# Rounds of half a batch with all heads, key products on VectorE, and weights decoded by integer bits, in a fused RWKV6 attention and MLP kernel

## The chip, the cores and the metric

The kernel runs on one core of one Trainium2 chip. The metric is the device time of one execution in microseconds (us), the median of several runs. A run over 1.5% above the fastest of its kernel is called slow, the others fast; only fast runs are compared, while medians and ranges given here are of all runs. A core has TensorE (matmuls), VectorE, ScalarE and GpSimd (elementwise work), and SyncE, which here issues transfers. In the profile they are PE (PEld is its weight load), DVE, ACT, POOL and SP. "L304" is line 304 of the kernel concerned; the kernel before and the changed one number their lines differently.

## The reference

Four batches, eight heads, 768 steps, 48 channels a head. The recurrence runs over the steps; its output, with the heads side by side, is the input x of a normalised two-layer MLP over 4 x 768 = 3072 tokens.

```python
for t in range(S):                       # per batch and head; state is 48 x 48
    cur = u * k[t] (outer) v[t]
    y[t] = r[t] @ (state + cur)
    state = w[t][:, None] * state + k[t] (outer) v[t]
x  = y.transpose(0, 2, 1, 3).reshape(B, S, H * D)          # 3072 x 384
xn = (x - mean(x)) / sqrt(var(x) + 1e-6) * g_ln
out = x + maximum(xn @ w_ch1, 0) @ w_ch2                    # 384 -> 1536 -> 384
```

The MLP weights reach the kernel as 64-bit floats, as pairs of 32-bit words, and are turned into 32-bit floats on the chip, in 24 pieces of 128 x 384.

## The kernel before

Attention is done in chunks of 64 steps. Inside a chunk six levels halve the steps: at level n the later half of each block reads from the earlier half (one set of matmuls, 96 in a round as the trace counts them), then R and K are multiplied by the decay products of their blocks. A unit is two heads by 768 steps, a round is two units. The levels of a round run beside the ends of the round before (kn transposes, states, outputs), the transposes of the round after, and pieces of the MLP as filler. The MLP of a batch needs all eight heads, hence two rounds.

```python
units = [(b, g) for b in range(B) for g in range(G)]      # g: a pair of heads, all 768 steps
...
    # a level, after its matmuls, for both units of the round
    POOL.tensor_tensor(out=K[:, :, 0, :], in0=K[:, :, 0, :], in1=T[:, :, 1]..., op=ALU.mult)   # L296
    DVE.tensor_tensor(out=R[:, :, 1, :], in0=R[:, :, 1, :], in1=T[:, :, 0]..., op=ALU.mult)    # L300
    # then copy_predicated (masked) from PSUM to A on VectorE, L313
...
    # decoding of one piece: exponent, mantissa, product
    DVE.tensor_scalar(out=e, in0=hi, ... shift 20, and 0x7FF)
    ACT.activation(out=e, in_=e, func=AF.Relu, bias=bias)                # bias -896
    DVE.tensor_scalar(out=e, in0=e, ... min 255, mult 2**23)
    DVE.scalar_tensor_tensor(out=e, in0=hi, ... sign bit, in1=e)
    DVE.tensor_scalar(out=m, in0=hi, ... and 0xFFFFF)
    ACT.activation(out=m, in_=m, func=AF.Copy, bias=1.0, scale=2.0**-20)
    DVE.scalar_tensor_tensor(out=m, in0=lo, scalar=2.0**-52, in1=m, ...)
    POOL.tensor_tensor(out=dst, in0=m, in1=e, op=ALU.mult)
...
    # the MLP of 384 tokens: statistics, 9 transposes, then the h matmuls and the o matmuls
    # (the trace counts 72 of each)
```

## Time and profile before

| What | Kernel before |
|---|---|
| time, median of 3 runs | 722.87 us (722.41 to 725.46) |
| first h matmul of the MLP | 193.2 us |
| from there to the end of the profiled span (724.5 us) | 531.3 us |
| busy: TensorE, VectorE, ScalarE, GpSimd | 616.1, 309.5, 190.0, 259.9 us |

The page gives the busy time of each engine and its course over 40 slices of the span; what matters here is the moment at which the MLP's first matmul can start, because from there on TensorE hardly ever waits. So I cut each profile at that matmul: the stretch from 20 us to it is called the start (the first 20 us are loads and set-up), the stretch behind it the rest. The prediction below shows the lines of before. The same cut at exactly the first h matmul; columns are the stretch, its length, then busy time (and instructions) of PE, PEld, DVE, ACT and POOL, the granted TensorE clock, DMA share and GB/s:

```profile
20.00:193.17 173.17, 96.40 (x2452) 83.00 (x2452) 145.55 (x260) 63.87 (x131) 125.72 (x130) 0.63 0.52 114
193.17:724.50 531.33, 505.80 (x5873) 325.83 (x5871) 159.22 (x348) 119.13 (x259) 115.33 (x127) 0.96 0.12 26
```

In the start TensorE is busy for 96 of 173 us, at a mean clock of 0.63; VectorE is busy for 146.

### The profile page before, as it was taken

To read this page: it belongs to the slowest core of one execution; us is meant where nothing else is said; L and a number is where in the kernel's file an instruction comes from. 1 tells how busy PE (TensorE), PEld (TensorE's weight loads), DVE (VectorE), ACT (ScalarE), POOL (GpSimd) and SP (SyncE) were. 2 spreads that over 40 slices of the span, in tenths; PEclk is the share of its full clock that TensorE was granted. 3 is DMA by queue.
4 is the path that set the end of the run, shared out by engine and by line. 5 is a ranking of instruction groups with operands and counts; after the bars stand their busy time and mean duration, and the time that the engine had idled before them with its cause. 6 is when DMAs were issued, how large, how long until landed. Compare 5 with 4: busy or idle time off the path is not lost.

```text
span 724.5 us, 18947 instructions
## 1 busy us (share of the span) xinstructions
PE 616.1 (85%) x8456; PEld 419.2 (58%) x8456; DVE 309.5 (43%) x612; ACT 190.0 (26%) x402; POOL 259.9 (36%) x301
## 2 busy tenths in 40 slices
PE   6632655568799989997999999999999999799998
PEld 4522545557456666676566666676666566455554
DVE  1479999896605332345306242556053012400000
ACT  3142453341522114213212241124210420220210
POOL 9975786775405142336104161533012100000000
PEclk9975565655799989997799999996999999999999
DMA  9919438532202330225002520000000000000000
GB/s 158 225 27 201 116 82 181 118 67 50 44 1 46 70 70 2 38 58 90 1 1 46 104 36 1 24 23 10 1 13 24 2 1 23 12 1 22 12 0 33
DMA packets 120688, 36.80 MB, mean 51 GB/s; under 512 B 114336, under 2 KB 117536, under 8 KB 120608
## 3 DMA queue, kind: packets, MB, share of 16 engines
q1 hardware_dynamic: 120608, 35.60, 24.2%
q8 instruction: 66, 1.08, 0.6%
q14 instruction: 14, 0.11, 0.1%
HBM read 30.87 MB, written 4.72 MB: 49 GB/s over the span
## 4 chain that ended last, share of the span: by engine, by line
PE 67%; DVE 19%; POOL 5%; issue 4%; ACT 3%; DMA 1%; POOLq 0%; SPq 0%; DVEq 0%
PE h_ps L429 25%; PE o_ps L439 23%; PE a_ps L286 9%; DVE rT L300 3%; DVE A L313 3%; DVE we L206 2%; DVE s L351 2%; PE xT_ps L420 2%; DVE wm L210 2%; DVE wm L214 2%; PE y L372 2%; DVE we L198 1%; DVE we L203 1%; PE y L382 1%; ACT A L311 1%
## 5 line engine op out<-in xcount | busy, mean ns | idle before, releaser
L429 PE MATMUL h_ps<-xT,w_sb 128*128 128x384 f32 x576 | 199.2, 506 | 1.3 <-ACT h L434 1.0
L439 PE MATMUL o_ps<-w_sb,h 128*128 128x384 f32 x576 | 193.3, 488 | 0.0
L296 POOL TENSOR_TENSOR kT<-kT,tot 128x384 f32<-128x384 f32 x80 | 89.3, 1128 | 207.3 <-PE a_ps L286 207.0
L429 PEld LDWEIGHTS h_ps<-xT,w_sb 128*128 128x128 f32 x576 | 112.2, 198 | 79.4 <-issue 8.0
L286 PE MATMUL a_ps<-rT,kT 48*64 48x32 f32 x4608 | 106.3, 247 | 58.3 <-DVE A L313 39.8
L439 PEld LDWEIGHTS o_ps<-w_sb,h 128*128 128x128 f32 x576 | 106.8, 190 | 68.2
L286 PEld LDWEIGHTS a_ps<-rT,kT 48*64 48x64 f32 x4608 | 97.6, 166 | 83.9 <-issue 57.8
L300 DVE TENSOR_TENSOR rT<-rT,tot 128x384 f32<-128x384 f32 x80 | 62.1, 780 | 148.0 <-PE a_ps L286 145.5
L434 ACT ACTIVATE h<-h_ps 128x384 f32<-128x384 f32 x96 | 46.7, 490 | 141.1 <-PE h_ps L429 141.1
L445 DVE TENSOR_TENSOR o<-o_ps,x 128x384 f32<-128x384 f32 x24 | 13.4, 557 | 164.4 <-PE o_ps L439 164.3
L313 DVE COPY_PREDICATED A<-mask,a_ps 128x384 f32<-128x384 int8 x80 | 55.1, 750 | 0.0
L351 DVE SCALAR_TENSOR_TENSOR s<-s,decay,kv 128x48 f32<-128x48 f32 x160 | 42.0, 263 | 4.7
L358 ACT COPY sx<-s 64x288 f32<-64x288 f32 x32 | 13.7, 430 | 100.3 <-DVE s L351 100.0
L217 POOL TENSOR_TENSOR w_sb<-wm,we 128x384 f32<-128x384 f32 x24 | 31.0, 1299 | 19.6 <-DVE wm L214 12.1
L372 PE MATMUL y<-v,A 64*64 64x48 f32 x384 | 26.9, 232 | 6.5 <-DVE s L351 5.3
L296 POOL TENSOR_TENSOR kT<-kT,wT 128x384 f32<-128x384 f32 x16 | 21.7, 1363 | 27.2 <-PE a_ps L286 19.7
L233 ACT COPY rT<-r_ps 128x384 f32<-128x384 f32 x32 | 13.9, 480 | 66.4 <-PE r_ps L229 41.7
L372 PEld LDWEIGHTS y<-v,A 64*64 64x64 f32 x384 | 24.7, 146 | 8.2 <-issue 8.2
L256 POOL TENSOR_TENSOR rk<-nat_k,nat_r 128x576 f32<-128x576 f32 x16 | 23.3, 1458 | 16.8 <-PE a_ps L286 8.2
L372 PE MATMUL y<-vx,A 64*64 64x48 f32 x384 | 26.3, 232 | 1.5 <-issue 1.5
L421 ACT ACTIVATE xT<-xT_ps,g_sb 128x384 f32<-128x384 f32 x24 | 13.1, 578 | 54.7 <-PE xT_ps L420 54.6
L342 PE MATMUL kv<-v,kn 64*64 64x48 f32 x768 | 19.6, 246 | 9.2 <-DVE s L351 5.4
(59 smaller groups left out, 652.5 us busy)
## 6 DMA issues: line engine op xcount, KB each, us to landing
raw<-in_moe_w_ch_dram SPq DMA_DIRECT2D x24, 384.0 KB, 4.5
nat_w<-in_w_dram SPq DMA_DIRECT2D x32, 144.0 KB, 3.9
nat_k<-in_k_dram SPq DMA_DIRECT2D x32, 144.0 KB, 3.5
nat_r<-in_r_dram SPq DMA_DIRECT2D x32, 144.0 KB, 4.2
v<-in_v_dram SPq DMA_DIRECT2D x32, 144.0 KB, 3.9
out_dram<-o SPq DMA_DIRECT2D x24, 192.0 KB, 1.9
vx<-in_v_dram SPq DMA_DIRECT2D x32, 72.0 KB, 3.5
u_bc<-in_u_dram SPq DMA_DIRECT2D x1, 192.0 KB, 4.3
```

The lines of the kernel that those rows point to most:

```text
L217: POOL.tensor_tensor(out=dst, in0=m, in1=e.bitcast(F32), op=ALU.mult)
L256: POOL.tensor_tensor(out=rk, in0=nat["k"][q % 2][:, :, :, 0:D], in1=nat["r"][q % 2][:, :, :, 0:D], op=ALU.mult,)
L286: PE.matmul(ps[ds(C * (i ^ j), C), j, u, c].rearrange("s (q n) -> s q n", n=n), K[rows, ts(m, C)], R[rows, m, :, 1, :], start=True, stop=True,
L296: POOL.tensor_tensor(out=K[:, :, 0, :], in0=K[:, :, 0, :], in1=T[:, :, 1][:, :, None].broadcast_to(blocks), op=ALU.mult,)
L300: DVE.tensor_tensor(out=R[:, :, 1, :], in0=R[:, :, 1, :], in1=T[:, :, 0][:, :, None].broadcast_to(blocks), op=ALU.mult,)
L313: DVE.copy_predicated(out=out_j[:, :, 1, :], mask=masks[lev], data=ps_j)
L342: PE.matmul(kv[ds(HP * j, HP), i, c], a["kn"][ds(C * i, C), c, ds(HP * j, HP)], vn[q][ds(C * i, C), c, j, :], start=True, stop=True,)
L351: DVE.scalar_tensor_tensor(out=s[:, m, :], in0=s[:, m - 1, :], scalar=a["T"][NLEV][:, m : m + 1], in1=new, op0=ALU.mult, op1=ALU.add,)
L372: PE.matmul(y[ds(C * i, C), j, c], A[rows, j, q % 2, c, :], vx[q][rows, c] if j else vn[q][rows, c, j], start=c == 0, stop=c + i == 0, ski ...
L429: PE.matmul(ps, w1_sb[:, kc, ts(f, P)], xT[:, kc, :], start=kc == 0, stop=kc == KC - 1,)
L434: ACT.activation(out=hs[f], in_=ps, func=AF.Relu)
L439: PE.matmul(ps, hs[f][:, ts(i, P)], w2_sb[:, f, :], start=f == 0, stop=f == FC - 1)
```

## The change

The intent: start the MLP after one round, not two, and take work off the two engines that hold up the start. A unit becomes four heads by 384 steps; two units, all eight heads, make a round that ends in 384 finished tokens. The state at step 384 is carried to the second half. The K products go from GpSimd to VectorE. Decoding works on the integer bits: ScalarE scales the absolute high word and converts the low word, VectorE clamps, shifts and sets the sign, and GpSimd adds the low bits as an integer. Further: unit 1's loads are issued by ScalarE, the mask copies move from GpSimd to ScalarE, raw weights come into three buffers of one piece, the three PSUM uses of attention share two buffers, and x rows are copied once per MLP to be contiguous.

```diff
-    units = [(b, g) for b in range(B) for g in range(G)]
+    rounds = [(b, f) for b in range(B) for f in range(NHALF)]
+    units = [(b, f, g) for b, f in rounds for g in range(U)]
...
+    load(0)
+    load(1, ACT)
...
-            POOL.tensor_copy(
+            ACT.copy(
                 out=half[rows],
...
-            e = ph.tile([P, WC], I32, tag="h", name=f"we{i}")
-            m = ph.tile([P, WC], F32, tag="h", name=f"wm{i}")
+            e = p3.tile([P, WC], I32, tag="we", name=f"we{i}")
+            low = p2.tile([P, WC], I32, tag="wl", name=f"wl{i}")
+            ACT.activation(
+                out=e.bitcast(F32), in_=hi.bitcast(F32), func=AF.Abs, scale=2.0**-16
+            )
+            ACT.activation(out=low, in_=lo, func=AF.Copy, scale=2.0**-29)
             DVE.tensor_scalar(
-                out=e, in0=hi, scalar1=20, scalar2=0x7FF,
-                op0=ALU.logical_shift_right, op1=ALU.bitwise_and,
-            )
-            ...
+                out=e.bitcast(F32), in0=e.bitcast(F32), scalar1=2.0**-31,
+                scalar2=1.875 - 2.0**-23, op0=ALU.max, op1=ALU.min,
+            )
+            DVE.tensor_scalar(
+                out=e, in0=e, scalar1=3, scalar2=0x7FFFFFF8,
+                op0=ALU.logical_shift_left, op1=ALU.bitwise_and,
+            )
             DVE.scalar_tensor_tensor(
                 out=e, in0=hi, scalar=-(1 << 31), in1=e,
                 op0=ALU.bitwise_and, op1=ALU.bitwise_or,
             )
-            ...
-            POOL.tensor_tensor(out=dst, in0=m, in1=e.bitcast(F32), op=ALU.mult)
+            POOL.tensor_tensor(out=dst.bitcast(I32), in0=e, in1=low, op=ALU.add)
...
-            POOL.tensor_tensor(
-                out=K[:, :, 0, :], in0=K[:, :, 0, :],
-                in1=T[:, :, 1][:, :, None].broadcast_to(blocks), op=ALU.mult,
-            )
-            DVE.tensor_tensor(
-                out=R[:, :, 1, :], in0=R[:, :, 1, :],
-                in1=T[:, :, 0][:, :, None].broadcast_to(blocks), op=ALU.mult,
-            )
+            for nm, i in (("r", 1), ("k", 0)):
+                X = a[nm].rearrange("p (q two n) -> p q two n", two=2, n=n)[:, :, i, :]
+                DVE.tensor_tensor(
+                    out=X, in0=X, in1=T[:, :, 1 - i][:, :, None].broadcast_to(blocks),
+                    op=ALU.mult,
+                )
...
+            DVE.tensor_copy(out=xn[i], in_=x[:, :, i, :])
```

## The prediction

> **What bounds the kernel now.** First I read the page: busy shares, and the 40 slices (18.1 us each).
>
> ```profile
> PE 616.1 (85%) x8456; PEld 419.2 (58%) x8456; DVE 309.5 (43%) x612; ACT 190.0 (26%) x402; POOL 259.9 (36%) x301
> ...
> PE   6632655568799989997999999999999999799998
> ...
> DVE  1479999896605332345306242556053012400000
> ...
> POOL 9975786775405142336104161533012100000000
> PEclk9975565655799989997799999996999999999999
> ```
>
> There are two stages. In slices 2 to 10 TensorE is busy half the time, at half clock in places, while VectorE reads 9. From slice 11 TensorE reads 9. The busy times of the engines in three stretches give the cut exactly; the columns are the stretch, its length, then PE, PEld, DVE, ACT and POOL busy, then PEclk:
>
> ```profile
> 20.00:192.00 172.00, 95.23 (x2446) 82.25 (x2445) 144.38 (x258) 63.52 (x130) 124.55 (x130) 0.64 0.53 115
> 192.00:623.00 431.00, 409.79 (x5577) 269.46 (x5575) 154.70 (x337) 104.27 (x229) 116.50 (x127) 0.95 0.14 29
> 623.00:724.50 101.50, 97.18 (x305) 57.12 (x305) 5.69 (x13) 15.21 (x31) 0.00 (x0) 0.98 0.03 12
> ```
>
> So 192 us pass before the first MLP matmul; then 431 us of TensorE at 95%; then 101 us of pure MLP. The chain that ended last gives MLP prices (start, us, what):
>
> ```profile
> 193.24 23.08 PE h_ps L429 x66
> ...
> 649.22 23.23 PE o_ps L439 x72
> 674.30 23.49 PE h_ps L429 x72
> ```
>
> 384 tokens cost 23.5 + 23.2 + 2.5 (nine transposes with evacuations) = 49 us of TensorE, eight times: 394 us that no reordering removes. Attention, from the same chain at full clock, costs per round of 1536 head-steps in two units: 6 levels x 1.53, 36 transposes of w, k, r x 0.152 = 5.5, kn 1.6, kv 1.7, y 2.6; about 20.6 us, eight times.
>
> The first stage is where time lies. TensorE there waits for VectorE:
>
> ```profile
> 60.87 2.79 PE L286 MATMUL a_ps<-rT,kT 48*64 48x32 f32 x96 [17.55 <-DVE A L313]
> ```
>
> and VectorE is slowed by GpSimd. In the order of time of VectorE, the same 384-element instruction of weight decoding takes 0.35 us, or 1.15 when a GpSimd product runs:
>
> ```profile
> 46.52 0.35 DVE L198 TENSOR_SCALAR we<-raw 128x384 int32<-128x384 int32 x1
> 46.79 1.15 DVE L210 TENSOR_SCALAR wm<-raw 128x384 int32<-128x384 int32 x1
> 47.86 0.35 DVE L198 TENSOR_SCALAR we<-raw 128x384 int32<-128x384 int32 x1
> 48.13 0.35 DVE L210 TENSOR_SCALAR wm<-raw 128x384 int32<-128x384 int32 x1
> ```
>
> ```profile
> 46.67 1.05 POOL L217 TENSOR_TENSOR w_sb<-wm,we 128x384 f32<-128x384 f32 x1 [0.96 <-DVE we L206]
> ```
>
> The slow one ends at 47.94, just after the GpSimd product ended at 47.72.
>
> **What the Trainium skill says.** "SBUF — State Buffer", section "SBUF: two separate sides": VectorE and GpSimd share a port pair under an exclusive lock, held for a whole instruction, against VectorE operations in a two-port mode or with two SBUF inputs. The lines above agree. "VectorE: DVE Perf Modes", section "The perf-mode tier table": fp32 tensor_scalar in SBUF runs at twice the rate of tensor_tensor. The trace agrees: start to start 0.27 us against 0.47. "TensorE: Matmul & The Clock Gate", section "What's actually happening": TensorE's clock halves after an idle window of some 3.4 us. The trace agrees: a level's 96 matmuls take 1.53 us warm, but 2.79 after that wait of 17.55.
>
> **The change, part by part.** *Rounds.* A unit becomes four heads by 384 steps in place of two by 768. Instruction counts per round hardly change, but a round ends in 384 tokens, so the first MLP starts after one round and four levels, not two rounds and five levels. In the built order the first h matmul of before comes behind rounds 0, 1 and levels 0 to 4 of round 2; in the changed kernel behind round 0 and levels 0 to 3 of round 1. One round and one level, 20.6 + 1.5 = 22 us of TensorE, move from the starved stage to the full one. Their time is not removed; the starved time is.
>
> *Weights.* Before, one of 24 pieces costs VectorE three tensor_scalars and two two-input operations: 3 x 0.27 + 2 x 0.47 = 1.75 us uncontended. After: two and one, 1.0 us. ScalarE keeps two operations (now ahead of VectorE's) and GpSimd its one. It saves 18 us of VectorE in all.
>
> *K products.* 96 instructions leave GpSimd:
>
> ```profile
> L296 POOL TENSOR_TENSOR kT<-kT,tot 128x384 f32<-128x384 f32 x80 | 89.3, 1128 | 207.3 <-PE a_ps L286 207.0
> ...
> L300 DVE TENSOR_TENSOR rT<-rT,tot 128x384 f32<-128x384 f32 x80 | 62.1, 780 | 148.0 <-PE a_ps L286 145.5
> ```
>
> They take 111 us there (with 16 more of 1363 ns) and should cost VectorE 96 x 0.47 = 45. A level's chain from matmul to matmul keeps its length: two K products in series on GpSimd were 2.3 us, four products on VectorE are 1.9. What goes is 111 us of lock holding. Three copies per MLP (x to contiguous rows) add 24 x 0.27 = 6.5 us of VectorE. Its total falls near 300 us, no bound over the whole span.
>
> **Time to the first MLP.** Before, I price the VectorE instructions between 20 and 192 us at their uncontended spacing: weights 42, R products 37 x 0.47 = 17, mask copies 30 x 0.47 = 14, states 10, the rest 11: 94 us. They were busy 144. So 124.5 us of GpSimd cost 50 us, 0.40 for each.
>
> After, the built order puts in front of the first normalised rows: 17 weight pieces 17.5, 36 products 17, 16 mask copies 7.5, states 5.1, the rest 6: 53 us. GpSimd holds about 45 us beside it (18 weight additions, the own-term and decay products): 0.40 x 45 = 18. VectorE waits for levels another 14, an estimate: nine levels, mostly in the first three, which have no filler.
>
> The start itself gets worse. ScalarE issues unit 1's twelve loads before its first evacuation, then does ten mask copies, and the order puts a weight conversion, hence a DMA of weights, in front of unit 0's fourth evacuation. SyncE issues 26 loads before that DMA; at the 0.5 to 0.9 us each of this trace and some waits it lands near 24 us. Level 0's products, at 19.5 us before, move to about 28. With weight work from 25: 25 + 53 + 18 + 14 = 110, and 5 to the first h matmul: 115 us, against 193.
>
> **Sum.** Before, from the first h matmul to the end: 724.5 - 193 = 531.5. Add the 22 moved: 553.5. Handovers to a new MLP (outputs, statistics, transposes) happen eight times, not four, but each of before also had an inner one, and the levels of the running round lie between. I count 2.5 to 5 us each, and compare with the 21 us of TensorE idle in the full stage of before: no net change. 115 + 553.5 = 668.5 us, minus the 1.6 by which the span exceeds the median time: 667.
>
> **Rivals.** *The start stays VectorE- and GpSimd-bound.* GpSimd keeps 24 weight additions, squeezed into half the time, and the blocking per piece may rise. If VectorE loses as much per unit of work as before (144/94), and idles as before, 53 x 1.85 = 98 gives a first h near 130 and 682 us. *Weights arrive late.* Three buffers of one piece each, refilled through one in-order queue; six w2 pieces are fetched only after round 1's outputs. At some 3 us a piece that fits under the 24 us of the first h matmuls; at 5 us TensorE would stand 10 us, giving 677. *Handover becomes the bound.* Each MLP now needs fresh outputs of both units, and VectorE's queue interleaves statistics with level products. If each costs 6 us more with the clock dropping, 7 x 6 = 42 gives 709; the slack of one MLP ahead that before had inside a batch is gone. The order shows 10 us of attention matmuls around each, against it. *Better than I think:* levels on one engine shorten each chain and contention vanishes; first h at 95 us, 647.
>
> **Range and chances.** Start 100 to 130, full stage -8 to +15: 645 to 697. Only the handover rival or a wait I have not seen loses the 41 us to the 2% line at 708.4: faster 0.94, same 0.05, slower 0.01.
>
> **What would show it.** First h matmul near 115 us; VectorE near 300 us in all and its R and K products near 0.55 us, not 0.78, once weights are done; GpSimd about 150; TensorE 93% or more busy from the first h on; the last pure MLP about 50 us long. Wrong would be: waits of over 5 us before each MLP's transposes, a long wait of ScalarE for weights at the start beyond 30 us, or TensorE waiting for w2 near 140 us.

## The result, and the profile after

| | before | after |
|---|---|---|
| time, median (range), runs of this comparison | 724.16 us (722.41 to 725.46), 4 runs | 667.23 us (660.99 to 669.11), 4 runs |
| first h matmul | 193.2 us | 108.7 us |
| the rest | 531.3 us | 557.0 us |
| busy: TensorE, VectorE, ScalarE, GpSimd | 616.1, 309.5, 190.0, 259.9 us | 603.3, 300.4, 193.3, 145.4 us |

The ratio is 0.92, with a 95% interval of 0.9135 to 0.9265. Such a ratio here and below is the mean time of one kernel's fast runs over that of the other's in the same rounds, so it is not quite the ratio of the medians quoted. For two runs below, old_start and lock_reads, the recorded ratio works out only if a run is counted that the list of runs calls slow (678.02 and 681.90) and the profiled run is left out; the fast runs in their lists average 666.5 and 672.2 us, ratios near 0.918 and 0.925.

The page of the changed kernel, its busy shares and the 40 slices (16.6 us each):

```profile
PE 603.3 (91%) x8456; PEld 408.2 (61%) x8456; DVE 300.4 (45%) x683; ACT 193.3 (29%) x412; POOL 145.4 (22%) x195
...
PE   1785477999999999999999999999899989997997
...
DVE  1589897736721486016731565035801491133000
...
POOL 5837664540133004030133004030003000000000
PEclk9995576999999996999899998999999978998999
```

The reader is to see that the full row of nines of TensorE begins at slice 7 (counted from 0), where before it began at slice 11, and that GpSimd never reads 9 any more. The cut at the first h matmul, columns as above:

```profile
20.00:108.69 88.69, 61.19 (x1346) 50.89 (x1347) 77.02 (x151) 41.90 (x90) 52.67 (x54) 0.71 0.60 143
108.69:665.70 557.01, 538.01 (x7096) 354.67 (x7095) 219.93 (x529) 143.72 (x309) 81.48 (x111) 0.96 0.17 38
```

The start shrinks by 84.5 us and VectorE's work in it by 68.5, GpSimd's by 73. The rest grows by 25.7 us: 1223 more matmuls (7096 against 5873) lie in it. That is the exchange of the plan: the work moved behind the first h matmul runs at TensorE's pace.

The products of a level, in the groups of the changed kernel (operands in partitions x elements; count; busy us and mean ns; idle of VectorE before them):

```profile
L304 DVE TENSOR_TENSOR kT<-kT,tot 128x384 f32<-128x384 f32 x80 | 53.2, 666 | 0.0
L304 DVE TENSOR_TENSOR rT<-rT,tot 128x384 f32<-128x384 f32 x80 | 49.8, 623 | 128.5 <-PE a_ps L294 128.0
```

The R products fall from 780 to 623 ns each, and the K products take 666 on VectorE, where GpSimd needed 1128.

How many matmuls lay ahead of the first h matmul? These are the groups of before in the stretch that ends there:

```profile
L286 PE MATMUL a_ps<-rT,kT 48*64 48x32 f32 x1824 | 52.5, 277 | 55.9 <-DVE A L313 39.1 <-DVE s L349 8.4 <-POOL kT L296 5.4
L342 PE MATMUL kv<-v,kn 64*64 64x48 f32 x210 | 7.4, 306 | 9.2 <-DVE s L351 5.4 <-ACT kn L331 3.8
L330 PE MATMUL kn_ps<-ident,kT 128*128 128x128 f32 x30 | 7.0, 399 | 0.6 <-POOL kT L296 0.6
```

and the same three of the changed kernel:

```profile
L294 PE MATMUL a_ps<-rT,kT 48*64 48x32 f32 x960 | 27.6, 275 | 5.8 <-DVE kT L304 5.6 <-DVE A L317 0.2
L348 PE MATMUL kv<-v,kn 64*64 64x48 f32 x96 | 3.3, 307 | 1.6 <-DVE s L360 1.6
L334 PE MATMUL kn_ps<-ident,kT 128*128 128x128 f32 x12 | 3.3, 430 | 9.5 <-ACT kn L335 5.7 <-DVE kT L304 3.8
```

At 96 a level, before did 19 levels first and the changed kernel does 10. TensorE's waits for VectorE's masked copies, 39.1 us in before, are 0.2 us in the changed kernel.

### The profile page after: what moved, and what is told of

It reads as the page before. It is cut to its first block, busy times and chain, and to the rows that moved or that the text cites. A ratio compares the mean times of both kernels' runs of the same rounds, so it can differ in the third digit from the quotient of the medians.

```text
span 665.7 us, 19173 instructions
## 1 busy us (share of the span) xinstructions
PE 603.3 (91%) x8456; PEld 408.2 (61%) x8456; DVE 300.4 (45%) x683; ACT 193.3 (29%) x412; POOL 145.4 (22%) x195
## 3 DMA queue, kind: packets, MB, share of 16 engines
q1 hardware_dynamic: 118368, 34.73, 23.8%
## 4 chain that ended last, share of the span: by engine, by line
PE 79%; DVE 11%; issue 3%; DMA 3%; ACT 2%; POOL 1%; SPq 1%; ACTq 0%; DVEq 0%; POOLq 0%
PE h_ps L448 29%; PE o_ps L457 28%; PE a_ps L294 9%; PE xT_ps L439 2%; PE kv L348 2%; DVE kT L304 2%; DVE rT L304 2%; PE w_ps L232 2%; DVE A L317 2%; PE kn_ps L334 2%; PE r_ps L232 1%; PE k_ps L232 1%; PE y L387 1%; DVE stats L426 1%; PE y L403 1%
## 5 line engine op out<-in xcount | busy, mean ns | idle before, releaser
L304 DVE TENSOR_TENSOR rT<-rT,tot 128x384 f32<-128x384 f32 x80 | 49.8, 623 | 128.5 <-PE a_ps L294 128.0
L464 DVE TENSOR_TENSOR o<-o_ps,x 128x384 f32<-128x384 f32 x24 | 13.4, 559 | 123.7 <-PE o_ps L457 123.7
L275 POOL TENSOR_TENSOR vo<-v,own 128x576 f32<-128x576 f32 x16 | 19.8, 1239 | 178.2 <-DMA v<-in_v_dram 165.4
L304 DVE TENSOR_TENSOR kT<-kT,tot 128x384 f32<-128x384 f32 x80 | 53.2, 666 | 0.0
L360 DVE SCALAR_TENSOR_TENSOR s<-s,decay,kv 128x48 f32<-128x48 f32 x160 | 29.4, 258 | 25.4 <-PE kv L348 25.4
L250 POOL TENSOR_TENSOR tot<-wT 128x384 f32<-128x384 f32 x16 | 14.8, 926 | 110.5 <-DVE kT L304 110.5
L220 POOL TENSOR_TENSOR w_sb<-we,wl 128x384 int32<-128x384 int32 x24 | 28.5, 1196 | 33.3 <-DVE we L216 24.7
L259 POOL TENSOR_TENSOR rk<-nat_k,nat_r 128x576 f32<-128x576 f32 x16 | 26.3, 1644 | 41.7 <-DMA nat_r<-in_r_dram 16.0
L369 ACT COPY sx<-s 64x288 f32<-64x288 f32 x32 | 13.8, 430 | 73.7 <-DVE s L360 73.4
L335 ACT COPY kn<-kn_ps 128x384 f32<-128x384 f32 x32 | 14.0, 481 | 52.3 <-PE kn_ps L334 38.9
L232 PE MATMUL k_ps<-ident,nat_k 128*128 128x128 f32 x96 | 18.7, 341 | 10.5 <-ACT wT L236 10.5
L439 PE MATMUL xT_ps<-ident,xn 128*128 128x128 f32 x72 | 18.7, 373 | 10.1 <-DVE xn L431 9.0
L403 PE MATMUL y<-sx,rx 48*64 48x48 f32 x384 | 24.5, 222 | 1.8 <-issue 1.8
```

The costliest lines, as they stand in the source:

```text
L220: POOL.tensor_tensor(out=dst.bitcast(I32), in0=e, in1=low, op=ALU.add)
L232: PE.transpose(ps[:, ts(c, P)], nat[nm][q % 2][:, pr * TT + c].rearrange("p j d -> p (j d)"), ident,)
L259: POOL.tensor_tensor(out=rk, in0=nat["k"][q % 2][:, :, :, 0:D], in1=nat["r"][q % 2][:, :, :, 0:D], op=ALU.mult,)
L304: DVE.tensor_tensor(out=X, in0=X, in1=T[:, :, 1 - i][:, :, None].broadcast_to(blocks), op=ALU.mult,)
L360: DVE.scalar_tensor_tensor(out=s[:, pr, m, :], in0=s[:, pr, m - 1, :] if m else before[:, pr, 2 * TT - 1, :], scalar=a["T"][NLEV][:, c : c ...
L403: PE.matmul(y[ds(C * i, C), j, k_], R, s, start=False, stop=True, skip_group_check=True,)
```

## The experiments

Twelve more runs were made, of eleven further kernels and of the changed kernel again, all with correct results. Each was compared with the kernel before in the same rounds on the same chip (medians of before in the four batches of runs: 724.98, 725.51, 725.7 and 723.98 us). This table sums up what each profile showed; "clock's loss" is explained under the last experiment. Remarks behind # in the diffs below are mine, and each diff is cut to its main lines.

| kernel | median us (range) | ratio, 95% interval | first h | rest | clock's loss in the rest | rest less loss |
|---|---|---|---|---|---|---|
| before | 724.16 (722.41 to 725.46) | | 193.2 | 531.3 | 21.7 | 509.6 |
| changed | 667.23 (660.99 to 669.11) | 0.92, 0.9135 to 0.9265 | 108.7 | 557.0 | 19.9 | 537.1 |
| k_only | 723.58 (720.96 to 724.56) | 0.997, 0.9945 to 0.9994 | 187.0 | 535.9 | 23.8 | 512.1 |
| decoding_only | 708.44 (707.21 to 709.67) | 0.9761, 0.9727 to 0.9796 | 175.5 | 531.0 | 21.0 | 510.0 |
| old_rounds | 708.96 (704.89 to 710.37) | 0.9771, 0.9736 to 0.9806 | 169.6 | 536.3 | 26.0 | 510.3 |
| old_decoding | 683.29 (682.77 to 685.75) | 0.9433, 0.9412 to 0.9454 | 121.9 | 559.6 | 15.0 | 544.6 |
| k_on_pool | 676.02 (667.04 to 679.51) | 0.9247, 0.9192 to 0.9302 | profile slow | | | |
| old_start | 668.66 (662.25 to 678.02) | 0.9256, 0.9181 to 0.9332 | 111.6 | 548.9 | 9.6 | 539.3 |
| wl_three | 661.92 (659.97 to 664.32) | 0.9122, 0.9081 to 0.9163 | 105.9 | 556.7 | 20.5 | 536.2 |
| add_on_dve | 674.29 (668.02 to 675.04) | 0.9272, 0.9221 to 0.9323 | 105.4 | 567.9 | 29.2 | 538.7 |
| lock_reads | 677.62 (671.08 to 687.06) | 0.9325, 0.9263 to 0.9387 | 118.7 | 550.6 | 11.0 | 539.6 |
| lock_writes | 674.28 (673.98 to 678.59) | 0.9293, 0.9259 to 0.9327 | 121.5 | 551.3 | 14.1 | 537.2 |
| start_wl | 663.72 (658.4 to 675.15) | 0.9115, 0.9069 to 0.9161 | 108.8 | 555.5 | 17.1 | 538.4 |
| after_again | 667.91 (663.81 to 674.92) | 0.9204, 0.9166 to 0.9242 | 109.3 | 557.4 | 17.0 | 540.4 |

### Which part of the change carries the gain

**k_only**: the kernel before with its K products on VectorE, nothing else.

```diff
-            POOL.tensor_tensor(
+            DVE.tensor_tensor(
                 out=K[:, :, 0, :], in0=K[:, :, 0, :],
```

> The kernel before with only its K products moved to VectorE. Theory 1: 37 K products before the first MLP add 17 us to VectorE and take 43 us from GpSimd, which is 0.40 x 43 = 17 us of blocking less: no change of the start, 0.4 us a level shorter chains, 714 to 726 us. Rival 2 (GpSimd's lock is the main cost of the start): first h matmul at 170 us or earlier, 702 or less. Rival 4 (VectorE is the bound, and gets more work): 735 or more.

Its start, columns as before:

```profile
20.00:187.00 167.00, 102.79 (x2442) 87.61 (x2441) 148.54 (x293) 63.05 (x131) 92.25 (x92) 0.88 0.54 119
```

GpSimd lost 33.5 us (125.72 to 92.25) and VectorE, with some 33 more instructions, gained only 3.0 (145.55 to 148.54). At 0.40 us of VectorE for each us of GpSimd that is 13.4 us given back against 15.5 us of new products (33 x 0.47), so +2, near the 3.0 measured. The first h matmul comes 6 us earlier, but the rest is 4.6 us longer, and the time hardly moves, by 1.4 us in the median (ratio 0.997). The K move is near an even trade by itself.

**decoding_only**: the kernel before with the new decoding alone.

```diff
             e = ph.tile([P, WC], I32, tag="h", name=f"we{i}")
-            m = ph.tile([P, WC], F32, tag="h", name=f"wm{i}")      # and the old five VectorE instructions
+            low = ph.tile([P, WC], I32, tag="h", name=f"wl{i}")    # and the new three, as in the change
```

> The kernel before with only the new decoding of weights. Theory 1: 24 x 0.75 = 18 us of VectorE less before the first MLP, GpSimd as before: first h matmul near 175 us, the whole near 705 (700 to 712). Rival (decoding fits in gaps): 716 or more.

```profile
20.00:175.49 155.49, 102.63 (x2443) 87.81 (x2441) 116.29 (x212) 60.66 (x131) 116.23 (x130) 0.63 0.60 127
```

It is 17.1 us faster than before (708.44 against 725.51 in its rounds). First h comes at 175.5, 17.7 earlier, and the rest is unchanged at 531.0. The start's VectorE time fell by 29 us (to 116.29), more than the 18 us that the two instructions fewer a piece take when alone. That fits instructions that are not there not being held up either (145.55 busy for 94 uncontended in the prediction's count is a factor 1.55, and 18 x 1.55 = 28); but GpSimd's busy time in the start fell too, by 9.5 us (125.72 to 116.23), and the run does not separate the two.

**old_rounds**: the two together in the old rounds, that is the change without its rounds.

```diff
-            POOL.tensor_tensor(                                      # K products, as in k_only
+            DVE.tensor_tensor(
                 out=K[:, :, 0, :], in0=K[:, :, 0, :],
-            m = ph.tile([P, WC], F32, tag="h", name=f"wm{i}")        # decoding, as in decoding_only
+            low = ph.tile([P, WC], I32, tag="h", name=f"wl{i}")
```

> The kernel before with the K products on VectorE and the new decoding: only the rounds and the start differ from the changed kernel. Theory 1: VectorE work before the first MLP is 94 - 18 (decoding) + 17 (K) = 93 us, GpSimd 124.5 - 37 x 1.16 = 82, times 0.40 = 33; 126 us busy against 144, idle as before 28: first h matmul near 175 us, the whole near 706 (698 to 712). So rounds would carry some 40 of the 57 us. Rival 2 (moving K off GpSimd carries the gain): 680 or less.

```profile
20.00:169.58 149.58, 90.56 (x2442) 77.89 (x2440) 130.99 (x245) 61.06 (x131) 88.08 (x92) 0.67 0.63 132
```

708.96 us, no better than decoding_only: first h comes 5.9 us earlier, and the rest is 5.3 longer. So the distance to the changed kernel, 42 us, goes to the rounds and to what came with them: the small changes of the start, which old_start below finds worth nothing, and the raw-weight buffers, the shared PSUM buffers and the contiguous copies of x, which no run tests apart from the rounds.

**old_decoding**: the changed kernel with the decoding of before, the exponent in three buffers and the mantissa in two.

```diff
-            low = p2.tile([P, WC], I32, tag="wl", name=f"wl{i}")    # and the new six instructions
+            m = p2.tile([P, WC], F32, tag="wl", name=f"wm{i}")      # and the old eight
```

> The changed kernel with only the old decoding of weights (five VectorE operations a piece for three). Theory 1: 17 pieces before the first normalised rows at 0.75 us more each, 13 us, with the same GpSimd work; first h matmul near 121 us, the whole near 680 (675 to 686). Rival (VectorE has slack at the start and waits for levels, so decoding fits in gaps): under 672. Rival 3 (weights are what the first MLP waits for): ScalarE and VectorE in turn make a piece longer, w2 comes late and TensorE stands near 140 us: 690 or more.

```profile
20.00:121.89 101.89, 63.99 (x1348) 52.87 (x1347) 93.34 (x181) 41.31 (x86) 51.86 (x54) 0.71 0.59 133
```

VectorE needs 16.3 us more in the start than in the changed kernel (93.34 against 77.02), first h comes 13.2 later, and the time is 16 us longer. The decoding is worth 16 to 17 us in either form of the rounds.

**k_on_pool**: the changed kernel with the K products back on GpSimd.

```diff
-                DVE.tensor_tensor(
+                (POOL if nm == "k" else DVE).tensor_tensor(
```

> The changed kernel with only its 96 K products put back on GpSimd. Theory 1 (VectorE time before the first MLP is the sum of uncontended instructions plus 0.40 us for each us of GpSimd work beside it): up to the first h matmul 18 K products leave VectorE, 18 x 0.47 = 8.5 us less, and GpSimd gains 18 x 1.15 = 21 us, which costs VectorE 0.40 x 21 = 8.4: the two cancel. A level's chain gets 2.3 instead of 1.9 us, nine levels, 4 us. First h matmul at 109 to 116 us (108.7 now), the whole 667 to 676 us. Rival 2 (lock holding by K products is what made the old start slow, so moving them is the main part of the gain): the start goes back by 20 us or more, the whole to 690 or above.

The fast runs give 0.9247, against 0.92 and 0.9204 for the changed kernel in two batches; the intervals overlap. Only two of its four runs are fast; they average 670.3 us, where the changed kernel's average 666.1 and 667.1 in its two batches. Rival 2 (690 or more) is out, but whether the K move gains those 3 to 4 us in the new rounds, or nothing, is not settled.

### What bounds the start

**old_start**: the changed kernel with unit 1's loads on SyncE behind unit 0's, and the mask copies on GpSimd.

```diff
-    load(1, ACT)
+    load(1)                       # behind the load of u
-            ACT.copy(
+            POOL.tensor_copy(
```

> The changed kernel with the start of before: unit 1's loads issued by SyncE and not by ScalarE, the ten mask copies on GpSimd. ScalarE evacuates the first transposes from about 5.5 us and not from 17. The built order then decodes weights only after level 4 of round 0. Theory 1 (the new start costs what level 0 loses): level 0's products at 18 to 20 us in place of 29, the first h matmul 6 to 9 us earlier, 658 to 662 us. Rival 5 (VectorE has the same sum of work whenever it starts, and the weights, decoded later, now come after the levels): first h matmul within 3 us of 108.7, 664 to 670 us.

```profile
20.00:111.60 91.60, 57.69 (x1255) 48.86 (x1252) 72.64 (x148) 37.89 (x80) 44.40 (x47) 0.98 0.57 136
```

The products of level 0 start at 21.9 us, where in the changed kernel they start at this line of VectorE's timeline:

```profile
29.03 0.87 DVE L304 TENSOR_TENSOR rT<-rT,wT 128x384 f32<-128x384 f32 x1 [1.18 <-PE a_ps L294]
```

So the first chain is 7 us earlier, and yet first h comes at 111.6, not before 108.7. What the queue of ScalarE delays at the very start is not what the first h matmul waits for. VectorE's busy time in the start is 4.4 us shorter (72.64 against 77.02), but its idle time is 7.3 us longer (91.60 - 72.64 = 19.0 against 11.7): 9.4 us of it are three waits for level matmuls, the two longest of them (3.0 and 4.7) just before the first weight is decoded, at 48.9. So the early start is given back as idle time; that the sum of VectorE's work alone sets the first h matmul is not shown. The ratio, 0.9256, does not differ from the changed kernel's.

**wl_three**: the changed kernel with three buffers for the low words. In the changed kernel this stands in the timeline:

```profile
72.41 0.56 ACT L207 ACTIVATE wl<-raw 128x384 int32<-128x384 uint32 x1 [6.66 <-POOL w_sb L220]
72.86 0.47 ACT L335 COPY kn<-kn_ps 128x384 f32<-128x384 f32 x1
...
73.39 0.90 PE L334 MATMUL kn_ps<-ident,kT 128*128 128x128 f32 x3 [5.70 <-ACT kn L335]
```

ScalarE stands 6.66 us before the low word's conversion, until GpSimd has added an earlier one and freed its buffer. Behind it in ScalarE's queue lies the evacuation of kn, for which TensorE waits 5.70 us. An instruction fed by the weights blocks the attention chain, with which it shares no data, because both are in one queue.

```diff
-            low = p2.tile([P, WC], I32, tag="wl", name=f"wl{i}")
+            low = p3.tile([P, WC], I32, tag="wl", name=f"wl{i}")
```

> The changed kernel with three buffers in place of two for the low words of the weights. In the trace of the changed kernel ScalarE stands 6.7 and 4.7 us before the first MLP for GpSimd's additions to free such a buffer, and the evacuation of the turned K, and TensorE with it (5.7 us), waits behind it. Theory 6 (that in-order wait is on the path): the first h matmul 4 to 8 us earlier, 659 to 663 us. Rival (VectorE's sum sets the start, the wait only moves idle time): 665 to 669 us.

```profile
20.00:105.87 85.87, 60.99 (x1347) 50.44 (x1347) 78.67 (x151) 42.37 (x90) 54.68 (x54) 0.72 0.61 148
```

First h is 2.8 us earlier, less than the 4 to 8 expected and less than half of the wait seen: VectorE is then idle for only 7.2 of 85.87 us, where it was for 11.7 of 88.69, and TensorE still waits 3.6 us for copies of kn at its w transposes (1.0 in the changed kernel). The ratio is 0.9122, against 0.92 and 0.9204. The fast runs average 662.0 us against 666.1 and 667.1, so 4 to 5 us, of which the profile shows the 2.8 in the start and nothing in the rest (556.7 against 557.0).

**add_on_dve**: the addition of the low bits on VectorE, to free GpSimd.

```diff
-            POOL.tensor_tensor(out=dst.bitcast(I32), in0=e, in1=low, op=ALU.add)
+            DVE.tensor_tensor(out=dst.bitcast(I32), in0=e, in1=low, op=ALU.add)
```

> The changed kernel with the 24 additions of the low words on VectorE and not on GpSimd (low bits of the weights may round otherwise; the result may lose some digits). Theory 1: 17 additions before the first MLP add 8 us to VectorE and take 18 us from GpSimd, 7 us of blocking: 665 to 670 us. Theory 6 (waiting for GpSimd to free buffers is on the path): ScalarE's two waits vanish too, 658 to 664 us. Rival (VectorE is the bound): 674 or more.

In the start GpSimd is busy for 28.39 us, not 52.67, and VectorE for 77.97 with 15 more instructions: as with the K products, what the addition costs VectorE comes back from GpSimd's silence. First h is 3.3 us earlier. But the time is 674.29, 7 us longer, since the rest takes 567.9 us. Of those 11 us more, 9 are the clock's loss (29.2 against 19.9); whether that belongs to this kernel or to its runs stays open, though all its runs lie at 668 or above. Both theories had named less; the time falls at the edge of the rival's range (674 or more), but not for the rival's reason, since the start did not get longer.

### What a microsecond of GpSimd costs VectorE

The prediction took 0.40 us from one division in one trace. Two kernels built on wl_three add GpSimd work that nobody needs, ahead of each of the 24 additions, into a tile that the addition then overwrites. As built, this work does not stay with the additions: the traces have all 24 products starting between 16.6 and 49.4 us, and all 72 memsets between 16.6 and 69.4, often several in a row. **lock_reads** adds a product of two SBUF operands:

```diff
+            ub = u_bc.rearrange("p h d -> p (h d)")
+            POOL.tensor_tensor(out=dst, in0=ub, in1=ub, op=ALU.mult)
             POOL.tensor_tensor(out=dst.bitcast(I32), in0=e, in1=low, op=ALU.add)
```

> The changed kernel with three low-word buffers, and on GpSimd one more product of 128x384 f32, read from SBUF, ahead of each of the 24 weight additions (some 17 to 18 of them before the first h matmul, about 1.05 us each: some 18 us of GpSimd, which then is busy some 73 of the 86 us between 20 us and the first h matmul, which the version without the extra products starts at 105.9). If a us of GpSimd that reads SBUF costs VectorE 0.40 to 0.43 us, as I reckoned, VectorE's busy time before the first h matmul grows from 78.7 to about 86, and the first h matmul moves by 5 to 10 us, to 111 to 116. Rival 1, the two only share a cause and the extra products cost VectorE nothing: VectorE stays within 2 us of 79, and h moves by less than 3 us. Rival 2, GpSimd is itself the chain that sets the start: h moves by the whole 18 us, to about 124, with VectorE idle longer and not busy longer. Time 667 to 673 by the theory, 662 by rival 1, 680 by rival 2.

**lock_writes** adds three memsets, which read nothing:

```diff
+            for _ in range(3):
+                POOL.memset(dst, 0.0)
             POOL.tensor_tensor(out=dst.bitcast(I32), in0=e, in1=low, op=ALU.add)
```

> The same, but with three memsets of the 128x384 f32 weight tile in place of the extra product (0.3 to 0.5 us each, so about as much GpSimd time, which writes SBUF and reads nothing). By what the Trainium skill's SBUF page states, VectorE instructions with two SBUF inputs are held up only by GpSimd instructions that read SBUF, while those in a two-port mode (the two tensor_scalars of a piece) are held up by any: so about half the cost of the run with products or less, VectorE 79 to 83 us busy before the first h matmul, which comes at 106 to 110. Rival, any GpSimd time costs VectorE alike: VectorE 85 to 87 us and h at 111 to 116, as with the products.

The start of lock_reads:

```profile
20.00:118.73 98.73, 63.53 (x1347) 52.72 (x1347) 83.94 (x151) 42.07 (x90) 71.77 (x77) 0.60 0.54 129
```

and of lock_writes:

```profile
20.00:121.51 101.51, 63.02 (x1346) 52.22 (x1347) 95.78 (x151) 42.18 (x90) 75.84 (x124) 0.94 0.54 126
```

With products, GpSimd is busy 17.1 us longer than in wl_three and VectorE, for the same 151 instructions, 5.3 us longer: 0.31 for each. First h moves by 12.9 us, more than the 5 to 10 expected; VectorE also idles 7.6 us more (14.8 against 7.2), most of it one wait of R products for GpSimd's decay products, 7.3 us. So both the waiting beside GpSimd and GpSimd's own queue count; my expectation had the first and left out the second. The two fast runs average 672.2 us, 10 more than wl_three's.

With memsets, VectorE is busy 17.1 us longer for 21.2 us of GpSimd, 0.81 for each: twice the rate of the prediction, where I had expected less than from products. The timeline of lock_writes shows how:

```profile
60.60 0.77 POOL L221 MEMSET w_sb<- 128x384 f32 x2
61.00 0.55 DVE L216 SCALAR_TENSOR_TENSOR we<-raw,we 128x384 int32<-128x384 int32 x1
...
62.40 3.75 DVE L208 TENSOR_SCALAR we<-we 128x384 f32<-128x384 f32 x1
62.63 3.30 POOL L221 MEMSET w_sb<- 128x384 f32 x9
```

Nine memsets run in a row, and a tensor_scalar that takes 0.35 us alone ends 0.2 us after the last of them, after 3.75. The longest of them, at 45.76, takes 8.21 us; it ends 0.2 us after a run of 27 memsets (43.96 to 53.75). The two-input instruction at 61.00 takes 0.55 beside a memset, as it does alone. Over the start, these first tensor_scalars average 1241 ns (567 in wl_three), mostly because of these two (their median is 400); the two-input instructions with the sign average 608 (618 in wl_three). The R and K products with the decay products, which have two inputs too, average 937 (698 and 787 in wl_three); but each of those over 1 us ran beside a GpSimd instruction that reads SBUF, such as the one of 1.37 us at 59.71 beside an addition from 59.66, and the R product at 30.15, wholly beside memsets, took 0.56. The Trainium skill, "SBUF — State Buffer", section "SBUF: two separate sides", makes this distinction: VectorE operations in a two-port mode wait for any GpSimd operation, those with two SBUF inputs only for one that reads SBUF. The trace agrees. (The prediction's short form of it leaves out the last condition.) What it does not say is that a tensor_scalar gets no turn between nine memsets.

So "0.40 us per us of GpSimd" is a mean over a mix of instructions, which holds for this kernel (see below) and is no constant: 0.31 and 0.81 were measured here with other mixes. And 0.81 is no rate of a memset either: of the 17.1 us, 12.1 are the first tensor_scalars' (22.2 against 10.1), 5.8 the R and K products' (28.1 against 22.3), which met other GpSimd work than in wl_three.

### The better version, and the scatter of the times

**start_wl**: old_start and wl_three together.

```diff
-    load(1, ACT)
+    load(1)                       # behind the load of u
-            ACT.copy(
+            POOL.tensor_copy(
-            low = p2.tile([P, WC], I32, tag="wl", name=f"wl{i}")
+            low = p3.tile([P, WC], I32, tag="wl", name=f"wl{i}")
```

> The changed kernel with unit 1's loads on SyncE and the mask copies on GpSimd, as before the change, and three low-word buffers. Theory, the sum of VectorE's work sets the start and ScalarE's low-word wait adds some us: level 0 at 22 us, first h matmul at 104 to 109, time 657 to 664, no more than 3 us from the version with three buffers alone (661.9). Rival, with the buffer wait gone the 7 us of earlier level 0 are now worth something: first h matmul at 97 to 101 and 653 to 657.

663.72 us, ratio 0.9115 (0.9069 to 0.9161): it is level with wl_three, and the earlier level 0 again gains nothing, first h at 108.8. wl_three and start_wl are the fastest versions found, some 0.9% ahead of the changed kernel (0.9122 and 0.9115 against 0.9204, whose interval begins at 0.9166; the first comparison, 0.92, has the wider interval of 0.9135 to 0.9265, which overlaps). They never ran in one batch with the changed kernel, so the distance goes by way of the kernel before.

**after_again**: the changed kernel, with no edit (so no diff), to test a reading of the traces. The times of the new rounds scatter more than those of before: 661 to 669 us in one batch. In the changed kernel's trace, in short stretches around the start of the third MLP (columns as before):

```profile
246.00:247.00 1.00, 0.53 (x12) 0.52 (x13) 0.99 (x2) 0.01 (x1) 0.00 (x0) 1.00 0.41 81
...
248.00:249.00 1.00, 1.00 (x74) 1.00 (x66) 1.00 (x6) 0.23 (x1) 0.00 (x0) 0.88 0.78 150
249.00:250.00 1.00, 1.00 (x12) 0.94 (x8) 1.00 (x3) 0.00 (x0) 0.00 (x0) 0.50 0.38 66
250.00:259.00 9.00, 9.00 (x116) 6.62 (x115) 5.47 (x13) 3.32 (x8) 2.35 (x2) 0.50 0.69 129
259.00:264.00 5.00, 5.00 (x11) 2.67 (x11) 3.89 (x5) 1.01 (x2) 2.83 (x3) 0.66 0.52 97
264.00:269.00 5.00, 5.00 (x17) 2.91 (x16) 0.75 (x1) 1.47 (x3) 1.78 (x2) 1.00 0.00 0
```

TensorE waits 1.03 us for a masked copy (until 246.5); 2.3 us later the clock falls to half (a mean of 0.88 over 248 to 249 puts the fall at 248.8), and stays there some 13 us although TensorE is busy throughout. The 0.66 of 259 to 264 puts its return at about 262.4, 3.7 us after the h matmuls of this MLP begin (258.7). The same handover in old_start's trace:

```profile
245.00:269.00 24.00, 22.67 (x349) 15.71 (x341) 13.55 (x33) 8.14 (x18) 6.82 (x5) 1.00 0.54 102
```

Full clock. I summed one minus the granted clock over stretches of 2 us behind the first h matmul, from the next even microsecond on; this is the "clock's loss" of the table. (Begun at the first h matmul itself, the sums are 0.2 to 0.9 us larger.) It lies between 9.6 and 29.2 us, mostly at the starts of MLPs, where level, transposes and MLP change over.

> The changed kernel unchanged, once more, to test a reading of the traces so far: that the scatter of its times comes from how long TensorE runs at half clock after the handovers. In the eight runs in the new rounds whose profile fell in the fast state, the time after the first h matmul lies between 548.9 and 567.9 us, and what the half clock took (the sum of one minus the granted clock) between 9.6 and 29.2; the difference of the two lies between 535 and 545, about 538 for this version of the weights. If the reading holds: first h matmul at 108 to 110 us, the rest less the clock's loss at 535 to 540 whatever the time of the run, ratio to the kernel before 0.914 to 0.927. Rival, the scatter is slower work of any kind (transfers, waits): the rest less the clock's loss varies with the time, outside 533 to 542 if the run's span differs by over 5 us from the earlier 665.7. And if three low-word buffers are worth 5 us, this kernel's ratio stays above 0.915, where that version had 0.912; below 0.913 they are worth nothing.

First h came at 109.3, the rest less the clock's loss is 540.4: at the edge of what the reading expected (535 to 540), inside the rival's limits, and the span, 666.7, differs too little from 665.7 to tell them apart. The table says more. In the four profiles with the old rounds the rest varies from 531.0 to 536.3 and, less the clock's loss, from 509.6 to 512.1; in the changed form with the new decoding (eight profiles) it varies from 548.9 to 567.9 and, less the loss, from 536.2 to 540.4. So most of the scatter of the rest is the time at half clock. On the start the clock has no such hold: over the start its mean is 0.71 in the first profile of the changed kernel and 0.93 in this one, and first h comes at 108.7 and 109.3. And the ratio, 0.9204, is above the 0.915 that the expectation set for three low-word buffers being worth something. What decides whether a handover drops the clock no run here shows.

## Why the prediction was right

The time was 667.23 us against 667.0 predicted. By its own steps that is closer than it deserves: the start was 6.3 us shorter and the rest 3.5 us longer than it said, so the span came out 2.8 us shorter (665.7 against 668.5). The last step then had the wrong sign. The prediction took 1.6 us off because the span of before, 724.5, exceeds the median time of 722.87; but that profile belongs to a run of 726.54 us, 2.0 more than its span, and the changed kernel's to one of 667.42, 1.7 more. That the two errors cancel is luck. (The lower end of its range is 644 by its own sums, 100 + 545.5 - 1.6, not 645.)

**The start (115 predicted, 108.7 measured).** Level 0's products were put at 28 and came at 29.0. The chain was 25 + 53 + 18 + 14 + 5. In the trace VectorE begins decoding at 22.0, so the first term was 3 us too large. From 22 to 106.0, where the first transposes of the MLP start, it is busy 73.7 us and idle 10.3, where I had 71 busy and 14 idle: 84 against 85. The uncontended sum of 53 came out as 52 when I priced the executed instructions in the same way, and the contention as 22 beside 50 us of GpSimd, 0.43 each where I took 0.40. The last term was 2.7, not 5. That the late level 0 costs little was an assumption that old_start and start_wl bear out.

**Decoding.** The saving of 18 us of VectorE was right in kind, and in effect worth 17 us by decoding_only and 16 by old_decoding.

**K products.** I called the trade 45 us more on VectorE against 111 us of lock holding. k_only shows VectorE's start moving by +3.0 us, where those two rates give +2, and no time to speak of. VectorE's total was put near 300 and is 300.4, GpSimd's near 150 and is 145.4.

**Rounds and the rest (553.5 predicted, 557.0 measured).** The step that failed in size is "One round and one level, 20.6 + 1.5 = 22 us of TensorE, move from the starved stage to the full one". I had put the first h matmul of before behind rounds 0, 1 and levels 0 to 4 of round 2, that is 17 levels. The groups of the trace show 19, with part of the next round's kn and kv. Against the 10 of the changed kernel 9 levels moved, with 36 transposes of w, k, r, 18 kn transposes, 114 kv matmuls and one round of y. At the prediction's prices: 9 x 1.53 + 5.5 + 18/12 x 1.6 + 114/96 x 1.7 + 2.6 = 26.3 us. The rest less the clock's loss grew from 509.6 to 537.1, by 27.5 (26.9 if the sums begin at the first h matmul). The clock's loss itself is nearly the same in both, 21.7 and 19.9. The "no net change" of the handovers was not exact in TensorE's idle time: in the rest it fell from 25.5 to 19.0 us, while TensorE's busy time grew by 32.2.

**Rivals.** *The start stays bound* (first h near 130) fell: VectorE's contention factor in the start was 73.7/52 = 1.42, not the 1.53 of before, and it idled less. *Weights late* fell: no wait of TensorE for weights is among its waits. *Handover becomes the bound* was half seen: its waits stayed at most 4.7 us, and that one only at the last MLP, with nothing left beside it. Its clock drops do occur and are most of the scatter, but they cost before as much. *Better than I think* (647) fell: VectorE's contention is still there.

**The signs.** Right: TensorE 538.01/557.01 = 97% busy from the first h on; the last MLP, from its first transpose (611.2) to the end of its o matmuls (662.2), 51 us. Wrong: R and K products "near 0.55 us, not 0.78, once weights are done". From 200 us on those with the decay products still average 618 and 652 ns, while those with w itself, at level 0, take 552. GpSimd's own-term and decay products still run then, and hold up some of them: a K product at 209.38 took 1.18 us beside a decay product that began at 209.14, and the three before it 0.55 or 0.56.

What I did not foresee is ScalarE's wait for the low-word buffer (6.66 us), worth 4 to 5 us of time by the fast runs of wl_three.

## What to carry to other kernels

When a pipeline's slow stage is bound by elementwise engines and its fast stage by TensorE, moving the border between them can pay more than speeding either up: here 42 of 57 us go to the new rounds and what came with them, though no matmul was saved. Count an engine's work in uncontended spacings first and add the sharing of VectorE and GpSimd as a measured rate, but take the rate from the same mix of instructions. And look at what each small conversion waits for in the queue of an engine that also evacuates PSUM: one more buffer was the cheapest gain here.

## What the Trainium skill lacked or had wrong

- "SBUF — State Buffer", section "SBUF: two separate sides": the rule of who blocks whom agrees with the instructions looked at here, but it gives no rate by which a mix of instructions on GpSimd lengthens VectorE's. Measured: 0.43 us of VectorE's time per us of GpSimd in the changed kernel's start, 0.31 for added products, 0.81 for added memsets; and tensor_scalars took 3.75 and 8.21 us beside nine and 27 memsets in a row, so the loser was not let in between instructions.
- "TensorE: Matmul & The Clock Gate", section "What's actually happening": it lets the clock fall after an idle window of some 3.4 us and recover after one of sustained work. In the changed kernel it fell 2.3 us after a wait of 1.03 us and stayed at half for some 13 us with TensorE busy throughout (247 to 264 us); in another run of nearly the same program it did not fall there. Small attention matmuls and transposes filled most of that stretch; which of that counts as activity, no run here shows. This is said of that passage, not of the whole page.
- No page that I read draws this consequence for the order of a kernel's instructions, that a conversion waiting for a buffer which GpSimd frees, placed in ScalarE's queue, holds up PSUM evacuations behind it: 6.66 us of wait on ScalarE became 5.70 us on TensorE.
